# Infini-attention with a token-mixing MLP on one core: block-diagonal memory by wide products, head factors by constant masks, and all engine orders written anew

## The chip, the core and the metric

The kernel runs on one core of a Trainium2 chip. A core has five engines with queues of their own, each strictly in order: TensorE (PE) multiplies matrices into PSUM, VectorE (DVE) and ScalarE (ACT) work on PSUM and SBUF, GpSimd (POOL) on SBUF alone, and SyncE (SP) issues transfers here. Engines wait for each other by semaphores. The metric is the device time of one execution in microseconds (us); a median of several runs is compared.

## The reference

There are S = 2048 tokens of width D = 448. A gate g = sigmoid(x . gate_w) mixes an attention branch a and an MLP branch b for each token. Cut to what matters:

```python
# a: 16 heads of 28, 4 segments of 512 tokens, a running memory M, z for each head
for s in range(4):
    p = softmax(qs @ ks.T * scale + causal_mask)
    a_dot = p @ vs
    a_mem = (phi(qs) @ M) / (phi(qs) @ z + 1e-6)       # phi(t) = t + 1 if t > 0 else exp(t)
    outs.append(gh * a_mem + (1 - gh) * a_dot)         # gh = sigmoid(beta), one factor for a head
    M, z = M + phi(ks).T @ vs, z + sum(phi(ks))
a = concat(outs) @ wo
# b: LayerNorm over D, then an MLP that mixes tokens (S -> 1792 -> S)
u = gelu(h.T @ w1 + b1);  b = (u @ w2 + b2).T
out = g * a + (1 - g) * b
```

## The kernel before

The program records about 1,300 operations with the tiles they read and write, and then puts them on the engines by a table, ORDER, that lists each engine's instructions by name (`word@banks` names the PSUM banks or buffers it takes, `u1-3*2` stands for u1-3 and u1-4, and `#1` is the second operation of that name). Semaphore waits follow from the tiles. So an order that is unlucky costs waits, and never a wrong result.

**Names in the orders.** A number after the name is a tile of 128 tokens, a segment, a head group (4 heads, each in a block of 32 partitions) or an attention unit u = 4 x segment + head group.

- PE: `lo../hi../pr..` are projections of k, q, v (a `lo` and a `hi` use half the rows each; `t` are the v tiles), `sc<p>_<f>` scores of a pair of units in five fills, always in banks 0 to 3; `pv<u>` weights times v; `mst<s>` phi(k).T v of a segment; `mem<u>` phi(q) times the memory; `wo<T>` the output projection; `u<ft>-<st>` and `y<T>-<ft>` the products of the MLP's first and second layer, each of 448 columns, which fill the time between the others.
- ACT: `exp` of four banks at once (L943), `ek/eq` exp of k and q, `cp..` copies out of PSUM (some are on DVE: an operation may have an alternative engine), `gt` the gate's tanh column, `gl` GELU.
- DVE: `pad` copies of weights into padded heads, `bns/bna/vpe/nmr/ln` LayerNorm, `mk/phk` and `mq/phq` the rest of phi, `ta/tm` transposes out of PSUM (L986, L984), `eps/rec/oa/om/ot` the normalised, mixed and transposed attention output, `ev/ag/fin` the exits of the MLP and the output.
- POOL: memsets, `rstd`, `mask` (the causal part of a fill, L946), `o` (the sum of both attention parts, L1001).
- SP: `ld..` loads (ldw1_k_part and ldw2_k_part fill a ring of three weight slots, L554), `dtx` transposing loads of x (L512), `gk/gq` gathers of the heads' last rows through DRAM (24 stores at L731, then `_h` loads at L736, which make up head group 3 of k and q), `tk` the transposes of phi(k) (L757), `out` stores (L1069).

**The memory.** `do_mst` (L808 on) accumulates 128 x 128 sums in one bank; `msta` keeps a running total in float32 (L832, L835), and four `mstc` products (L839) write the four 32 x 32 blocks on the diagonal of each head group's 128 x 128 matrix mst_sb, times a factor maskg, one instruction for each partition block and all four head groups. The rest of mst_sb is zeroed once by `msz0` (L588).

**The head factors.** `do_small` (L843 on) computes gh and 1 - gh from tanh (L860, L862), and for each of the four partition blocks writes a one (`mo`, L866), the gate (`mg`, L867) and the factor for the other part (`oc`, L871): twelve small DVE instructions.

Of the kernel before, what the change touches and what calls it, by code (L numbers as in the profile page):

```python
# [307 lines left out]
y5-13 loq3_2@12 prq3_2 mst2@0 prq3_2h y3-3*3 y6-0@6 y3-6*3 sc6_4@0123 lot12@47 prt12 y6-1 y3-9 prt13 y3-10*2 y6-2
y7-0@4 sc7_0@0123 y7-1 y3-12 y6-3 y3-13 y6-4*2 pv12@7 y6-6 y7-2 sc7_1@0123 y7-3 pv13@5 y7-4 wo8@7 y6-7*2 mem13@5
sc7_2@0123 y6-9*2 y7-5 mem12@7 y6-11 y7-6 wo10@5 y6-12 y7-7 y6-13 sc7_3@0123 y8-0@7*2 wo11@5 y8-2 y10-0@6 y8-3 y7-8  # L310
y8-4 sc7_4@0123 y11-0@5 y7-9 y10-1 y8-5 y7-10*2 y11-1 y10-2 y11-2 y8-6 y10-3 y8-7*2 y9-0@3 y10-4 y7-12*2 wo9@0 y9-1*2
mem15@1 y9-3 y10-5 y9-4*2 y13-0@0 y9-6 y13-1 y11-3 y8-9*2 y10-6*2 y11-4 pv15@4 y9-7*2 pv14@1 y8-11 y10-8 y9-9 y15-0@4
# [8 lines left out]
cpq1_0 cpk1_0 cpq1_1 ek0_0 cpv3 gt3 cpv4 tb cpv5 cpv2 gt5 gt2 cpv1 cpv0 gt4 cpv7 gt6 gt0 gt7 gt1 eq1_0 exp0_0@1 cpk2_2
exp0_1@5 cpk2_1 exp0_2@4 eq1_1 exp0_3@2 exp0_4@6 ek0_2 exp1_0@3 ek0_3 exp1_1@1 eq1_3 exp1_2@5 ek1_0 exp1_3@0 ek1_1
exp1_4@4 gl0 exp2_0@6 exp2_1@1 cpq2_0 exp2_2@5 ek1_3 exp2_3@4 cpq2_2 exp2_4@0 eq2_0 exp3_0@6 ek1_2 exp3_1@2 gl5 gt9
gt8 exp3_2@0 gt11 gt10 exp3_3@3 ek2_0 exp3_4@4 eq2_2 exp4_0@2 exp4_1@5 eq2_1 exp4_2@3 eq2_3 exp4_3@1 exp4_4@6 gl10
exp5_0@0 exp5_1@5 ek2_2 ek2_1 exp5_2@1 eq3_1 exp5_3@2 eq3_0 exp5_4@6 ek2_3 exp6_0@3 exp6_1@4 exp6_2@5 exp6_3@7 cpv15
# [4 lines left out]
cpk0_1#1 gw bna0 maskg0 bna1 bna3 vpe0 cpk0_0#1 cpk0_1 cpq0_1 nmr0 cpq0_3 cpq0_0 bns6 bns4 ln3 bna4 bns7 bns5 bna5  # L330
bns8 bns11 bns10 bna8 bna11 ln1 bna6 bna7 vpe4 bns9 bns14 bna9 bna10 vpe8 ln0 bns15 bns13 nmr8 nmr4 mk0_0 ln4 ln2 cpv6
ln10 ln11 b2c b1c ln8 ln6 ln9 ln5 bns12 mo0 omgh cpk2_3 gh cpq2_3 ln7 mg0 bna13 bna12 bna15 oc0 bna14 oc1 mq1_0 vpe12
phk0_0 mq1_2 nmr12 oc2 ln14 gcol1 ln15 mk0_1 phk0_1 ln12 mo1 ln13 mg1 mo2 cpk2_0 mg2 oc3 ev1 gcol0 phq1_2 ev0 ta0 ev2
omg1 mk0_2 rec0 msz0 ta1 oa0 phk0_2 mq1_1 rec1 phq1_1 phq1_0 mk0_3 mo3 oa1 phk0_3 ev3 ev4 ta2 msta0 mk1_1 ev6 mk1_0
mg3 phk1_1 ot1 omg0 ot0 mq1_3 ta3 ev5 rec2 phk1_0 phq1_3 rec3 mstc0#3 mstc0#2 b2g0 cpq2_1 mstc0#1 mstc0 oa2 oa3 ev8
ev7 ot2 ot3 cpq2_2#1 tm4 mk1_3 eps4 ta4 ag0 rec4 ag2 oa4 ag1 ev9 mq2_0 ag3 mk1_2 cpv8 ta5 cpv9 tm5 phk1_2 eps5 b2g1
phk1_3 cpv11 rec5 om4 cpv10 oa5 tm6 ot4 phq2_0 om5 eps6 gcol2 mk2_0 ta6 rec6 ev10 oa6 phk2_0 tm7 omg2 mq2_2 eps7 om6
ta7 rec7 ev11 ot6 ev13 msta1 ot5 mstc1#3 ev12 om7 oa7 cpk3_1 cpk3_3 cpk3_0 ot7 cpq3_3 cpk3_2 cpq3_1 cpq3_0 mstc1#2 ag5
ag7 ag4 mq2_3 ag6 ta8 mstc1 mstc1#1 phq2_2 mq2_1 tm8 phq2_1 ta9 mk2_1 eps8 phk2_1 b2g2 rec8 oa8 phq2_3 tm9 om8 eps9
mk2_2 fin0 rec9 mq3_0 oa9 fin2 mk2_3 phk2_2 om9 phk2_3 ta10 fin1 tm11 tm10 ot8 eps11 ta11 fin4 ot9 mq3_1 phq3_0 eps10  # L340
cpv14 rec11 om11 oa11 fin5 rec10 msta2 om10 oa10 mstc2#1 cpv12 cpv13 ot10 ot11 mstc2#3 mstc2#2 mstc2 fin3 phq3_1 ta12
ta13 ag8 tm13 tm12 mq3_2 ag10 eps13 fin6 eps12 ag11 rec13 mq3_3 rec12 oa12 om13 oa13 om12 phq3_3 ag9 tm15 fin7 phq3_2
ta15 ot13 eps15 rec15 ta14 tm14 om15 eps14 rec14 oa14 om14 oa15 gcol3 ot15 omg3 b2g3 ot12 fin8 fin9 ot14 fin11 fin10
ag13 fin13 fin12 ag14 fin14 fin15 fin15#1
# [850 lines left out]
```

## Time and profile before

| what | value |
|---|---|
| median of 3 runs | 176.4 us (176.24 to 176.82) |
| the profiled execution | 176.64 us |
| its span, first to last instruction | 174.9 us |
| granted TensorE clock | 1.0 |
| ScalarE's exp of a fill, 40 times | 1.88 us each, 75.0 us |
| DMA moved | 24.66 MB, 141 GB/s on average |

Engine busy times overlap, so they don't add up to the span; what an engine's idle time is worth depends on who waits for it. Lines of the profile read: line of the kernel, engine, operation, output<-input, shape, count, then busy us and mean ns, then idle time before and who ended it.

### The profile page before, as it was taken

Reading aid. Unit: us, or ns where it says so; the run is one execution under the profiler, and the core shown is the slowest. Engines: PE = TensorE matmul, PEld = TensorE weight load, DVE = VectorE, ACT = ScalarE, POOL = GpSimd, SP = SyncE. Lnnn points to the kernel's source line nnn. Section 1 sums busy time; section 2 is a strip of 40 time slices with the busy share of each in tenths; the row PEclk is TensorE's granted clock in tenths of the full one; section 3 lists DMA queues with packets and bytes.
Section 4 is the critical chain, followed back from the end, with each engine's and each line's share of the span. In section 5 each row is a group of like instructions: output and inputs, shape, how many; then the busy total and the mean of one; then the engine's idle time right before and its main releaser. Section 6 shows DMA issues by size and latency. Waiting matters only on the chain.

```text
span 174.9 us, 5948 instructions
## 1 busy us (share of the span) xinstructions
PE 168.6 (96%) x2558; PEld 82.7 (47%) x2558; DVE 144.4 (83%) x336; ACT 118.9 (68%) x122; POOL 64.8 (37%) x93
## 2 busy tenths in 40 slices
PE   8799999999899999999999999999999999999993
PEld 3455444444346444454445344444454445565552
DVE  1788999899814997989897999998899889777963
ACT  2216998984899888999989897997667775000020
POOL 8020120653073005441745370856546242802200
PEclk9999999999999999999999999999999999999999
DMA  5989968948628974401256950047462651246133
GB/s 134 295 155 319 221 155 243 236 125 227 178 37 242 165 174 115 117 14 34 53 155 171 287 42 4 4 70 204 114 190 73 209 179 40 85 141 181 34 110 108
DMA packets 50474, 24.66 MB, mean 141 GB/s; under 512 B 14976, under 2 KB 50208, under 8 KB 50448
## 3 DMA queue, kind: packets, MB, share of 16 engines
q1 hardware_dynamic: 50160, 24.05, 54.5%
q8 instruction: 20, 0.33, 0.8%
q10 hardware_dynamic: 288, 0.23, 0.5%
q14 instruction: 6, 0.05, 0.1%
HBM read 18.76 MB, written 2.36 MB: 121 GB/s over the span
## 4 chain that ended last, share of the span: by engine, by line
PE 82%; DVE 11%; DMA 3%; issue 1%; SPq 1%
PE t L264 71%; PE t L934 6%; PE t L970 4%; DMA t<-in_A_x_dram 3%; DVE t L1007 2%; DVE t L1049 2%; DVE t L709 1%; PE t L819 1%; DVE t L720 1%; DVE t L986 1%; DVE t L839 1%; DVE t L1065 1%; SPq L502 0%; DVE t L614 0%; DVE t L779 0%
## 5 line engine op out<-in xcount | busy, mean ns | idle before, releaser
L264 PE MATMUL t<-t 128*32 128x448 bf16 (+9 forms) x1824 | 144.8, 346 | 0.9 <-DVE t L986 0.3
L264 PEld LDWEIGHTS t<-t 128*32 128x32 bf16 (+2 forms) x1824 | 66.9, 96 | 63.2 <-issue 11.0
L943 ACT ACTIVATE t<-t 128x2048 bf16<-128x2048 f32 x40 | 75.0, 1876 | 15.3 <-PE t L934 14.1
L946 POOL TENSOR_SCALAR_AFFINE_SELECT t<-t 128x512 bf16<-128x512 bf16 x64 | 42.7, 687 | 47.8 <-ACT t L943 46.9
L1001 POOL TENSOR_TENSOR t<-t 128x448 bf16<-128x448 f32 x12 | 14.3, 1197 | 27.2 <-DVE t L999 10.1
L934 PE MATMUL t<-t 28*128 28x512 bf16 (+3 forms) x256 | 15.8, 301 | 0.7 <-issue 0.7
L1027 ACT ACTIVATE t<-t 128x448 bf16<-128x448 f32 x2 | 1.4, 723 | 22.1 <-PE t L264 22.1
L1049 DVE TENSOR_SCALAR t<-t 128x448 bf16<-128x448 f32 x14 | 9.3, 662 | 7.8 <-PE t L264 7.8
L986 DVE STREAM_TRANSPOSE t<-t 128x512 f32<-128x512 f32 x16 | 11.1, 700 | 3.4 <-PE t L970 3.4
L1065 DVE SCALAR_TENSOR_TENSOR t<-t 128x448 bf16<-128x448 f32 (+2 forms) x17 | 10.8, 644 | 3.0 <-PE t L264 2.6
L885 POOL TENSOR_TENSOR t<-t 128x4 f32<-128x4 f32 x4 | 4.5, 1126 | 23.5 <-DVE t L883 23.5
L876 DVE BATCH_NORM_STATS2 t<-t 128x6 f32<-128x448 bf16 x16 | 9.3, 612 | 3.5 <-DMA t<-in_A_x_dram 3.5
L1007 DVE STREAM_TRANSPOSE t<-t 128x512 bf16<-128x512 bf16 x16 | 10.9, 693 | 1.2 <-POOL t L1001 1.2
L934 PEld LDWEIGHTS t<-t 28*128 28x128 bf16 x256 | 4.5, 92 | 15.4 <-ACT t L943 10.9
L1031 DVE TENSOR_SCALAR t<-t 128x448 bf16<-128x448 f32 x14 | 10.1, 736 | 1.9 <-PE t L264 1.9
L970 PE MATMUL t<-t 128*32 128x512 bf16 (+3 forms) x256 | 11.5, 299 | 0.0
L984 DVE STREAM_TRANSPOSE t<-t 128x512 f32<-128x512 f32 x12 | 8.4, 706 | 1.9 <-PE t L264 1.5
L970 PEld LDWEIGHTS t<-t 128*32 128x32 bf16 x256 | 6.8, 96 | 5.1 <-issue 0.4
L779 DVE SCALAR_TENSOR_TENSOR t<-t 128x512 bf16<-128x512 bf16 x12 | 9.0, 755 | 0.0
L997 DVE SCALAR_TENSOR_TENSOR t<-t 128x448 f32<-128x448 f32 x12 | 8.9, 742 | 0.1
L754 DVE SCALAR_TENSOR_TENSOR t<-t 128x512 bf16<-128x512 bf16 x12 | 8.2, 685 | 0.1
L774 ACT ACTIVATE t<-t 128x512 bf16<-128x512 bf16 x12 | 7.5, 626 | 0.7 <-DMA t<-spare_heads 0.7
(65 smaller groups left out, 122.5 us busy)
## 6 DMA issues: line engine op xcount, KB each, us to landing
t<-in_B_w_dram SPq DMA_DIRECT2D x52, 256.0 KB, 3.8
out_dram<-t SPq DMA_DIRECT2D x15, 112.0 KB, 3.0
t<-in_A_x_dram SPq DMA_DIRECT2D x3, 448.0 KB, 5.0
t<-in_B_w_dram SPq DMA_DIRECT2D x8, 128.0 KB, 2.7
t<-in_A_wo_dram SPq DMA_DIRECT2D x4, 98.0 KB
t<-in_A_wq_dram SPq DMA_DIRECT2D x1, 336.0 KB, 5.2
t<-in_A_wv_dram SPq DMA_DIRECT2D x1, 336.0 KB, 5.5
spare_heads<-t SPq DMA_DIRECT2D x8, 32.0 KB
```

Of the source, the lines that this page charges most:

```text
L264: last = e.matmul(out[q], w[:, q], x, skip_group_check=True, **kw)
L876: op("DVE", lambda e: e.bn_stats(st6[:, t, :], xh[:, t, :]), reads=[R_x[t]], writes=[R_st6[t]], name=f"bns{t}", cost=512, prio=P_PROJ - 10 ...
L934: last = e.matmul(bank(fb[hl])[:, c0 : c0 + w], kT[r, hg, s * 512 + j * 128 : s * 512 + j * 128 + 128], qT[r, hg, s * 512 + 128 * j : s * ...
L943: op("ACT", lambda e: e.activation(pslot(g), ps[:, fb[0].bank : fb[0].bank + 4, :], ACT.Exp, scale=SCALE), use=fb, reads=[bres(b) for b in ...
L946: op("POOL", lambda e, c0=c0: e.affine_select(pslot(g)[:, :, c0 : c0 + 128], pslot(g)[:, :, c0 : c0 + 128], pattern=[[0, 4], [1, 128]], co ...
L970: last = e.matmul(bank(cb)[32 * hl : 32 * hl + 32, 128 * j : 512], vaug[:, 4 * s + j, 32 * h : 32 * h + 32], pslot(P_fill[u // 2][f])[:, h ...
L986: dv(lambda e: e.transpose(t2[:, 0, :], bank(cb)[:, 0:512]), [bres(cb)], [R_tt[tb][0]], "ta", 630, use=(cb,))
L1001: op("POOL", lambda e: e.tensor_tensor(o3, n3[0], n3[1], op=ALU.add), reads=R_tt[tb], writes=[R_ob[tb]], name=f"o{u}", cost=1280, port=Tru ...
L1007: dv(lambda e: e.transpose(oT[:, hg, s * 512 : s * 512 + 512], o), [R_ob[tb]], qres(hg, s), "ot", 635)
L1031: alt=("DVE", lambda e: e.tensor_scalar(ag(T), bank(b)[:, 0:D], gcol[:, T : T + 1], b2g[:, T : T + 1], op0=ALU.mult, op1=ALU.add), dve_cos ...
L1049: alt=("DVE", lambda e: e.tensor_scalar_add(uT[:, ft, :], bank(b)[:, 0:D], b1c[:, ft : ft + 1]), dve_cost(448)))
L1065: op("DVE", lambda e: e.scalar_tensor_tensor(outst[:, p, c0:c1], bank(b)[:, 0 : c1 - c0], omg[:, T : T + 1], ag(T)[:, c0:c1], op0=ALU.mult ...
```

## The change

1. **Wide products.** maskg becomes a 128 x 4 x 4 x 32 tile that is zero off the diagonal blocks. Each `mstc` becomes one product of 128 x 512 that writes all of mst_sb for the segment, zeros too: `mstc0` straight from PSUM, `mstc1` and `mstc2` from the float32 total. `msz0` goes. mem waits for one instruction instead of four.
2. **Masks.** POOL builds a constant hmask (three memsets and two selections); `gm` and `osl` multiply the tanh column by it, `oc` becomes one reduction, `mg` one broadcast copy and `mo` one copy.
3. **Alternatives.** `pad`, `ln`, `mg` and `mo` may now run on ACT. In the new table padk1, padq0, padq1, ln1, ln11 and mo do; other copies out of PSUM change sides in both directions.
4. **One more buffer** for exp's results: NP from 5 to 6.
5. **All five orders** are new. The stem of each is as it was; SP's first 19 entries are the same.

The diff, cut to its core (the orders by the parts that are spoken of below):

```diff
     "PE": """
-warm@2 trx0_0@63 warm2 trx0_1@24 lok0_0@71 hik0_0 lok0_2@53 lok0_0h@20 hik0_2 hik0_0h loq0_1@67 gtr@4 lox0_3@03 hiq0_1
+warm@4 trx0_0@13 warm2 trx0_1@52 lok0_0@46 hik0_0 lok0_0h@25 lok0_2@07 hik0_0h loq0_1@13 hik0_2 lox0_3@52 gtr@4 hiq0_1
...
+sc1_0@0123 u3-6 u2-8 u3-7 u2-9 u3-8 u4-0@5 u2-10*2 u3-9 u4-1 u5-2 sc1_1@0123 u2-12 u5-3 u2-13 u4-2*2 u3-10 u2-14 u4-4
...
-u5-13 loq3_2@12 prq3_2 mst2@0 prq3_2h y3-3*3 y6-0@6 y3-6*3 sc6_4@0123 lot12@47 prt12 y6-1 y3-9 prt13 y3-10*2 y6-2
+sc7_0@0123 y7-3*2 y6-5 mst2@5 y6-6 pv12@7 y6-7 sc7_1@0123 y7-5 pv13@5 wo8@7 y6-8*4 y7-6 sc7_2@0123 y7-7 mem12@7 y7-8
...
     "ACT": """
-ldx1 ldwkb xTcp0_01 xTcp0_11 cpk0_2#1 cpk0_2 cpk0_3 cpq0_2 cpq1_2 cpk1_3 cpq1_3 ek0_1 cpk1_2 cpq1_2#1 cpk1_1 eq1_2
+ldx1 ldwkb padk1 xTcp0_01 xTcp0_11 padq1 cpk0_1 padq0 cpk0_1#1 cpk0_0 ek0_0 ek0_1 cpq1_2 ln1 cpq0_1 cpk1_2 cpk1_3
...
+cpk2_2 exp0_0@2 ln11 exp0_1@1 exp0_2@0 ek0_2 eq1_0 exp0_3@5 exp0_4@6 exp1_0@4 ek0_3 exp1_1@2 exp1_2@3 eq1_3 exp1_3@7
...
     "DVE": """
-bns0 padx2 wo0 xTcp0_00 padk0 padk1 padx1 padx0 padk2 bns2 xTcp0_10 bns1 cpk0_0 padq1 padq2 bna2 padq3 padq0 bns3 ob0
+bns0 ob0 padx2 xTcp0_00 maskg0 padx1 padk2 wo0 padx0 padk0 bna0 bns2 xTcp0_10 padq2 padq3 bns1 bna2 cpk0_0#1 bna1
...
+ln15 ln14 ln12 ln13 phk0_1 mq1_2 ev0 ev1 ta0 mk0_2 mq1_0 gcol1 phq1_1 mk0_3 phk0_3 rec0 mg phq1_2 ev2 phk0_2 oc oa0
...
-cpv14 rec11 om11 oa11 fin5 rec10 msta2 om10 oa10 mstc2#1 cpv12 cpv13 ot10 ot11 mstc2#3 mstc2#2 mstc2 fin3 phq3_1 ta12
+oa10 om10 mq3_0 cpq3_2 fin5 cpv14 om11 oa11 b2g2 cpv13 cpv12 fin3 mq3_1 ot11 msta2 ot10 ta12 phq3_0 mstc2 ag8 phq3_1
...
     "SP": """
-gk0_2 ldw1_3_0 gq0_1 ldw1_1_3 tk0_0 ldw1_3_1 gq0_3 tk0_1 gk0_1 ldw1_2_2 gk2_1 ldw1_2_1 ldw1_3_2 gk0_h0 gq0_h2 gk0_h1
-ldw1_2_3 gq0_h1 ldw1_3_3 ldwo3 gk2_0 gq0_h0 tk0_2 ldw1_4_1 tk0_3 ldw1_4_3 ldw1_4_0 ldw1_5_0 ldw1_4_2 ldw1_6_0 dtx3_0
+ldw1_0_0 dtx2_0 dtx2_1 ldw1_1_0 ldw1_0_1 gq0_3 gk0_2 gq0_0 gq0_2 ldwo0 ldw1_0_2 gk0_0 ldw1_0_3 gk0_3 gq0_1 tk0_0
+ldw1_3_0 ldw1_2_0 ldw1_2_1 gk0_1 gq0_h1 ldw1_1_1 gq0_h2 gq0_h0 ldw1_1_2 ldw1_2_2 tk0_1 ldwo2 gk2_0 gk2_2 gk0_h0 gk0_h1
+ldw1_1_3 gk2_3 ldw1_3_3 ldw1_4_1 ldw1_4_0 ldw1_3_1 tk0_3 gk2_1 ldw1_5_0 ldw1_2_3 ldw1_3_2 ldwo3 tk0_2 ldw1_4_2
...
+ldw2_1_3 gq2_h1 ldw2_2_0 ldw2_1_1 ldw2_2_2 gk3_0 ldw2_2_3 tk2_0 ldw2_3_0 ldw2_2_1 out0 ldw2_3_1 gk3_2 gk3_1 tk2_3 out2
...
-    NSL, NP = 3, 5
+    NSL, NP = 3, 6
...
-    maskg = sb([128, NHG, 32], F32)
+    maskg = sb([128, NHG, 4, 32], F32)
...
         if s == 0:
+            op("DVE", lambda e: e.tensor_tensor(diag(), wide(mps()), maskg[:], op=ALU.mult), use=(b,), ...
             op("DVE", lambda e: e.tensor_copy(mst_f32[:], mps()), ...
         else:
             op("DVE", lambda e: e.tensor_tensor(mst_f32[:], mps(), mst_f32[:], op=ALU.add), ...
-        for hl in range(4):
-            q = slice(32 * hl, 32 * hl + 32)
-            op("DVE", lambda e, q=q: e.tensor_tensor(mst_sb[q, s, :, q], mst_f32[q, :, :], maskg[q, :, :], op=ALU.mult), ...
+            op("DVE", lambda e: e.tensor_tensor(diag(), wide(mst_f32), maskg[:], op=ALU.mult), ...
...
+        for w, (v_, n_) in enumerate(((1.0, "hm0"), (0.5, "hm1"), (-0.5, "hm2"))):
+            dv(lambda e, w=w, v_=v_: e.memset(hmask[:, w], v_), [], [R_hmask], n_, "POOL")
...
+        for w, dst, r, n_ in ((1, gsel, R_gsel, "gm"), (2, osel, R_osel, "osl")):
+            dv(lambda e, w=w, dst=dst: e.scalar_tensor_tensor(dst[:], gh[:, :], 1.0 if w == 1 else -1.0, ...
+        dv(lambda e: e.tensor_reduce(omcol[:, :], ...
```

`wide(ap)` repeats the 128 x 4 x 32 input over the four blocks of a row, and `diag()` is mst_sb of the segment seen as 128 x 4 x 4 x 32.

More of the change, by code (lines that the diff above doesn't have):

```diff
@@ L308 @@
[L308 to L312, printed above, removed]
@@ L321 @@
[L321 to L325, printed above, removed]
@@ L330 @@
[L330 to L344, printed above, removed]
+bns0 ob0 padx2 xTcp0_00 maskg0 padx1 padk2 wo0 padx0 padk0 bna0 bns2 xTcp0_10 padq2 padq3 bns1 bna2 cpk0_0#1 bna1
@@ L476, in build_kernel @@
     R_v = R("v", NT)
-    R_mst = [R(f"mst{i}_", 4) for i in range(3)]
-    R_msz = R("msz")
+    R_mst = R("mst", 3)
     R_mstf, R_maskg = R("mstf"), R("maskg")
@@ L585, in build_kernel @@
     op("POOL", lambda e: e.memset(mhalf[:], -0.5), writes=[R_mhalf], name="mhalf", cost=200)
-    for t_, r_, n_, w_ in ((wo_sb, R_wo, "wo0", 896), (mst_sb, [R_msz], "msz0", 768), (maskg, [R_maskg], "maskg0", 128)):
+    for t_, r_, n_, w_ in ((wo_sb, R_wo, "wo0", 896), (maskg, [R_maskg], "maskg0", 512)):
         op("DVE", lambda e, t_=t_: e.memset(t_[:].bitcast(U32), 0), writes=r_, name=n_, cost=w_ / 0.96 + 10, prio=P_PROJ)
@@ L829, in mps, with wide, diag @@
             return bank(b)[:, 0:128].rearrange("p (g c) -> p g c", g=NHG)
+        def wide(ap):
+            return ap[:, :, None, :].to_broadcast([128, NHG, 4, 32])
+        def diag():
+            return mst_sb[:, s].rearrange("p g (l c) -> p g l c", c=32)
         if s == 0:
+            op("DVE", lambda e: e.tensor_tensor(diag(), wide(mps()), maskg[:], op=ALU.mult), use=(b,),
+               reads=[bres(b), R_maskg], writes=[R_mst[0]], name="mstc0", cost=dve_cost(512), prio=P_BASE)
             op("DVE", lambda e: e.tensor_copy(mst_f32[:], mps()), use=(b,), reads=[bres(b)], writes=[R_mstf], name="msta0",
@@ L836, in do_mst @@
                writes=[R_mstf], name=f"msta{s}", cost=dve_cost(128), prio=P_BASE)
-        for hl in range(4):
-            q = slice(32 * hl, 32 * hl + 32)
-            op("DVE", lambda e, q=q: e.tensor_tensor(mst_sb[q, s, :, q], mst_f32[q, :, :], maskg[q, :, :], op=ALU.mult),
-               reads=[R_mstf, R_maskg, R_msz], writes=[R_mst[s][hl]], name=f"mstc{s}", cost=dve_cost(128) + 10, port=True,
-               prio=P_BASE)
+            op("DVE", lambda e: e.tensor_tensor(diag(), wide(mst_f32), maskg[:], op=ALU.mult),
+               reads=[R_mstf, R_maskg], writes=[R_mst[s]], name=f"mstc{s}", cost=dve_cost(512), port=True, prio=P_BASE)
     def do_small():
@@ new lines, in do_small @@
+        for base, step in ((0, -32), (DH - 1, 32)):
+            dv(lambda e, base=base, step=step: e.affine_select(
+                hmask[:], hmask[:], pattern=[[0, 3], [0, NHG], [step, 4]], compare_op=ALU.is_ge, fill=0.0, base=base,
+                channel_multiplier=-1 if base else 1), [R_hmask], [R_hmask], "hs" + str(base), "POOL")
+        for w, dst, r, n_ in ((1, gsel, R_gsel, "gm"), (2, osel, R_osel, "osl")):
+            dv(lambda e, w=w, dst=dst: e.scalar_tensor_tensor(dst[:], gh[:, :], 1.0 if w == 1 else -1.0, hmask[:, w].rearrange("p g l -> p (g l)"),
+                                                              op0=ALU.add, op1=ALU.mult), [R_gh, R_hmask], [r], n_)
@@ new lines, in do_small @@
+        dv(lambda e: e.tensor_reduce(omcol[:, :], osel[:].rearrange("p (g l) -> p g l", l=4), axis=mybir.AxisListType.X,
+                                     op=ALU.add), [R_osel], [R_omcol], "oc")
+        for n_, io, rd in (
+            ("mg", lambda: (maskg[:, :, :, 0:DH], gsel[:].rearrange("p (g l) -> p g l", l=4)[:, :, :, None].to_broadcast([128, NHG, 4, DH])), R_gsel),
+            ("mo", lambda: (maskg[:, :, :, DH], hmask[:, 0]), R_hmask),
+        ):
+            op("DVE", lambda e, io=io: e.tensor_copy(*io()), reads=[rd, R_maskg], writes=[R_maskg], name=n_, cost=550 if n_ == "mg" else 100,
+               prio=pr, alt=("ACT", lambda e, io=io: e.activation(*io(), ACT.Copy), act_cost(448 if n_ == "mg" else 16, True)))
```

130 lines of the change are left out of this document (71 added, 59 removed).

## The prediction

> **What bounds the kernel now.** I read the page first: the span, the busy shares, the chain that ended last, the costliest groups.
>
> ```profile
> span 174.9 us, 5948 instructions
> PE 168.6 (96%) x2558; PEld 82.7 (47%) x2558; DVE 144.4 (83%) x336; ACT 118.9 (68%) x122; POOL 64.8 (37%) x93
> ...
> PE 82%; DVE 11%; DMA 3%; issue 1%; SPq 1%
> ...
> L264 PE MATMUL t<-t 128*32 128x448 bf16 (+9 forms) x1824 | 144.8, 346 | 0.9 <-DVE t L986 0.3
> ```
>
> TensorE is busy for 96% of the span and holds 82% of the chain; the change removes no matrix product (617 entries in PE's order before and after, the same names). So it can win only what TensorE does not fill. The windows of PE alone say where that is (window, length, busy, count, clock, DMA share, GB/s):
>
> ```profile
> 5.00:10.00 5.00, 3.88 (x53) 1.00 1.07 292
> 10.00:15.00 5.00, 4.71 (x55) 1.00 0.87 199
> 45.00:50.00 5.00, 4.34 (x32) 1.00 0.60 119
> 60.00:70.00 10.00, 9.94 (x108) 1.00 0.65 156
> 100.00:110.00 10.00, 9.88 (x189) 1.00 0.33 39
> 130.00:140.00 10.00, 9.68 (x166) 1.00 0.46 134
> 140.00:170.00 30.00, 30.00 (x576) 1.00 0.38 112
> ```
>
> Between 10 and 170 us PE idles 0.29 + 0.66 + 0.06 + 0.12 + 0.32 = 1.45 us, and in the last 30 us not at all. The gap in 5:10 is the wait for x (both orders issue those loads alike). A record hides part of each gap, so I measured the pace of starts. The group by form, then PE's timeline in two windows:
>
> ```profile
> L264 PE MATMUL t<-t 128*128 128x448 bf16 x214 | 46.6, 353 | 0.0
> ```
>
> ```profile
> 155.73 10.53 PE L264 MATMUL t<-t 128*32 128x448 bf16 x224
> ```
>
> ```profile
> 31.98 2.25 PE L264 MATMUL t<-t 128*128 128x448 bf16 x11
> 34.16 0.40 PE L934 MATMUL t<-t 28*128 28x512 bf16 x4
> 34.49 2.31 PE L264 MATMUL t<-t 128*128 128x448 bf16 x11
> ```
>
> 224 quarter products are 56 whole ones: 10.53 / 56 = 0.188 us each, while one record shows 0.353, so a gap of n shown stands for n + 0.165. A score of 512 columns should take 0.188 x 512 / 448 = 0.215; its start-to-start is 34.49 - 34.16 = 0.33. So a change of the array's tile shape costs 0.115 us. Counting shapes in the two order tables gives 97 changes before and 95 after.
>
> **The gaps, and what the change does to each.** (1) At the start, the timeline of 10.6 to 11.6:
>
> ```profile
> 10.68 0.48 DVE L565 MEMSET t<- 128x512 uint32 x1
> ...
> 11.08 0.36 DVE L709 CAST t<-t 128x256 bf16<-128x256 f32 x1
> ...
> 11.50 0.39 PE L264 MATMUL t<-t 64*128 64x512 bf16 x2 [0.29 <-DVE t L709]
> ```
>
> PE waits for a projection's bank, which DVE empties only after the memset ob0. Afterwards ob0 is second on DVE, that copy (the second cpk0_1) runs on ACT, and two products stand between the bank's filling and its reuse. The gap, 0.29 + 0.165 = 0.45, goes. What is late next: the copies of x for the third block (dtx2), wanted earlier, and ACT, which before the first exp gains three pads and one normalisation (ln1) and loses one exp (eq1_0) and some copies. I take 0.3 of 0.45; bounds -0.3 to 0.45.
>
> (2) At 46 us; SP's timeline, then all engines:
>
> ```profile
> 43.67 0.47 SPq L736 DMA_DIRECT2D t<-spare_heads  x1
> ```
>
> ```profile
> 44.25 1.86 ACT L943 ACTIVATE t<-t 128x2048 bf16<-128x2048 f32 x1
> ...
> 46.80 0.63 ACT L774 ACTIVATE t<-t 128x512 bf16<-128x512 bf16 x1 [0.69 <-DMA t<-spare_heads]
> ...
> 46.86 0.40 PE L934 MATMUL t<-t 28*128 28x256 bf16 x8 [0.66 <-issue]
> ```
>
> The exp that held the score banks ended at 46.11, yet both the score of unit 3 and ACT's eq1_3 start at 46.8: both read head group 3 of q, which the transfer gq0_h0 brings from DRAM, issued only at 43.67. It stood right behind gk2_0 in SP's order; now it stands five entries ahead of it, with gk0_h0 and gk0_h1 soon behind. Gain 0.66 + 0.165 - 0.115 (the change that is there anyway) = 0.71. I take 0.7; bounds 0 to 0.71.
>
> (3) At 137 us, DVE's timeline and PE's row:
>
> ```profile
> 135.31 0.88 DVE L839 TENSOR_TENSOR t<-t 32x128 bf16<-32x128 f32 x3
> ...
> 137.46 1.30 DVE L986 STREAM_TRANSPOSE t<-t 128x512 f32<-128x512 f32 x2
> ```
>
> ```profile
> 138.22 0.56 PE L264 MATMUL t<-t 128*32 128x448 bf16 x8 [0.32 <-DVE t L986]
> ```
>
> PE waits for a bank that ta12 empties; before it DVE wrote three of the four diagonal blocks, 0.88 us. Now mstc2 is one instruction and stands behind ta12. The gap, 0.32 + 0.165 = 0.49, goes. What is late next is mem12, which reads mstc2: mst2 is 6.2 us of product time later in PE's order and mem12 only 0.35 later (columns counted in both tables at the pace above). From mst2 to mem12, DVE has msta2 0.25, two transposes 1.4, phq3_0 0.68, mstc2 0.7: 3.0 us, against 3.9 us of products. I take 0.5; bounds 0 and 0.5.
>
> (4) Smaller waits on DVE: 0.06 and 0.12 shown, and others that the records hide. The list of waits:
>
> ```profile
> PEld t L264 <- DVE t L1049: 1.1, 4, 0.4
> ```
>
> Weight loads wait there four times and at a few more lines once or twice; five gaps hidden by 0.165 each and the 0.18 shown make 1.0 us at most. Whether they go hangs on DVE's load, so I price that. The rows by line:
>
> ```profile
> L839 DVE TENSOR_TENSOR t<-t x12: 236/282/289, 62.8 to 135.9; 32x128 bf16<-32x128 f32 x12
> ```
>
> ```profile
> L835 DVE TENSOR_TENSOR t<-t x2: 227/252/278, 96.0 to 130.6; 128x128 f32<-128x128 f32 x2
> ```
>
> ```profile
> L999 DVE TENSOR_TENSOR t<-t x12: 561/616/795, 81.6 to 158.7; 128x448 f32<-128x448 f32 x12
> ```
>
> ```profile
> L867 DVE COPY t<-t x4: 199/213/525, 29.6 to 57.7; 28x112 f32<-28x112 f32 x4
> ```
>
> ```profile
> L871 DVE COPY t<-t x4: 125/160/166, 29.9 to 37.7; 32x4 f32<-32x4 f32 x4
> ```
>
> ```profile
> L588 DVE MEMSET t<- x3: 165/698/805, 4.4 to 41.9; 128x896 uint32 x1, 128x128 uint32 x1, 128x768 uint32 x1
> ```
>
> The wide product is not in the trace. From 128 to 448 elements a product grows by (616 - 252) / 320 = 1.14 ns an element, so 512 take 0.69 us (ends: 0.28 if as a block, 0.795 as the longest of 448). Removed: 12 blocks x 0.28 = 3.4; four mg 1.15, four oc 0.61, msz0 0.70; two gate halves (the price of an oc each) and four tiny memsets 0.6 together: 6.4. Added: three wide 2.1; maskg's memset grows from 128 to 512 elements, 0.84 ns each, 0.3; mg whole, 448 elements (0.25 to 0.74; taken 0.55); gm, osl and the sum oc, 16 elements each, at 0.2: 3.6. DVE loses 2.8 of 144.4 us; the swaps with ACT balance (about 6 us each way). Of the 1.0 us I take 0.3; bounds 0 and 1.0.
>
> (5) Two changes of shape fewer: 0.2. (6) At nothing: POOL's five mask instructions (16 to 48 elements, under 0.3 each) lie in its free time before 12 us; the sixth buffer for exp (NP) lets ACT run ahead, and ACT is not the bound; ACT's 1.2 us more (pads, ln1, ln11, mo) lies in its 32% of idle time, except that ln11 waits for nmr8 with exp0_1 and so the third score behind it.
>
> Gains: 0.3 + 0.7 + 0.5 + 0.3 + 0.2 = 2.0 us.
>
> **What the new order adds.** Every queue is reshuffled, so new gaps come. Before, an order of this kind had some ten gaps, 2.6 us. I see tight places: sc0_0 (ACT's last gate column about 0.1 late by my estimate), ln11, mem12 (0.9 to spare), and SP's queue:
>
> ```profile
> SPq L757 <- DVE t L754: 10.0, 2, 8.7
> ```
>
> ```profile
> L757 SPq DMA_TRANSPOSE t<-t x12: 1190/1228/3255, 31.4 to 122.5; - x12
> ```
>
> ```profile
> DMA to landing us min/median/max: 2.2/3.6/6.8
> ```
>
> (the last for L554, the weights). SP's transposes of phi(k) wait for DVE, longest 8.7 us, and what stands behind waits too. tk0_1 used to stand after ldw1_1_3; now ldw1_1_3 stands six entries behind tk0_1 (ldwo2, gk2_0, gk2_2, gk0_h0 and gk0_h1 between): 1.23 + 2.5 us of issues, then 3.6 to land. I put all new gaps together at 1.0 us; ends 0 and 3.1 (the slower rival below).
>
> **Sum.** The profiled execution took 176.64 us: span 174.9 and 1.7 around it, which the change leaves. 176.64 - 2.0 + 1.0 = 175.6. That execution is 0.24 above the median of the runs, 176.4; on the median the forecast is **175.4**.
>
> **Rivals.** *Nearly all is won*: new gaps of 0.2 or less: 176.4 - 1.8 = 174.6. For it: DVE lighter by 2.8. Against: the margins above are under 1 us.
>
> *Taken back elsewhere*: the gaps move, 2.0 new for 2.0 gone: 176.4. The likeliest place is the meeting of DVE and POOL:
>
> ```profile
> L995 DVE TENSOR_SCALAR t<-t x12: 142/172/615, 70.7 to 157.5; 128x16 f32<-128x16 f32 x12
> ```
>
> An instruction of 172 ns took 615: 0.44 lost, four or five such meetings in places that matter make 2.0. The Trainium skill, "SBUF — State Buffer", Who interferes with whom, says that a DVE instruction with two SBUF inputs contends with a GpSimd instruction that reads SBUF, and that whichever comes first keeps the pair for its whole length. By that rule mstc1 and mstc2, wide and with two such inputs, could each wait out a mask; the row of L839, the same kind in small, has 289 as its longest and bears no sign of it, while that of L995 agrees.
>
> *Slower: a weight behind a transpose.* ldw1_1_3 feeds u2-12, right behind the second score of pair 1. In the chain of waits that score is
>
> ```profile
> 43.50 0.33 PE t L934 x8
> ```
>
> and 1.1 us fewer products stand ahead of it now; with 0.3 won at the start it comes near 42. phk0_1, which releases tk0_1, and its neighbour on DVE:
>
> ```profile
> 34.04 0.69 DVE L754 SCALAR_TENSOR_TENSOR t<-t 128x512 bf16<-128x512 bf16 x1
> ...
> 34.65 0.71 DVE L892 TENSOR_SCALAR t<-t 128x448 bf16<-128x448 bf16 x1
> ```
>
> It ended at 34.73; afterwards 5.7 us of rows that stood ahead of it stand behind or elsewhere and 2.2 come ahead (two normalisations, copies), but DVE waits for PE in between, so I estimate 33.75. Then the weight lands at 33.8 + 3.7 + 3.6 = 41.1, 0.9 before its use: from 34.7 on, or with a landing above 4.5 of the 2.2 to 6.8, every 0.1 us late is 0.1 of PE. Two meetings with POOL (0.71 for a normalisation of 0.39 is one: 0.3) and a landing 1.0 longer make 0.6 + 1.0 - 0.9 = 0.7 of gap; the same pattern at two more transposes (tk0_3 before ldw1_2_3, tk2_0 before ldw2_2_1) makes 2.1 in all: 176.4 - 1.0 + 2.1 = 177.5.
>
> *The change doesn't do what it says*: if the wide products cost 0.795 and mg 0.74, DVE still loses 2.3; the case lies inside the forecast.
>
> **Chances.** Forecast (174.9 to 175.9) 0.40; nearly all won 0.20; taken back 0.22; slower 0.18. About 0.3% (0.53 us) is what a measurement of this kernel can tell from no change. Forecast and full gain lie beyond it: 0.60 faster; of "taken back", centred on no change, nearly all is within: 0.21; slower 0.19. The range from 174.0 to 177.2 cuts the lower edge of the full gain and the upper half of the slower case.
>
> **What would show it.** Right: no PE gap at 11 us, none with a release by the gather near 46, none before wo8; L839's successors three at about 0.69; DVE's busy time near 141.6; PE idle in 10 to 170 near 0.7 us. Wrong: a PE gap released by a DMA of L554 near 42 us, SP waiting longest on L754's successor; exp0_1 late behind ln11; mem12 late behind mstc2; POOL or DVE instructions at twice their usual length just before a PE gap.

## The result and the profile after

The changed kernel takes **175.17 us** in the median of 20 runs (174.49 to 176.5), the kernel before 176.51 us beside it (20 runs). The ratio is 0.9936 (95% interval 0.9911 to 0.996): 0.4 to 0.9% faster. The forecast was 175.4. The profiled execution took 175.05 us, against 176.64 before.

The page of the changed kernel: span, busy times, chain, and the largest group on TensorE.

```profile
span 173.3 us, 5628 instructions
PE 166.6 (96%) x2401; PEld 83.3 (48%) x2408; DVE 143.0 (83%) x314; ACT 120.2 (69%) x125; POOL 64.6 (37%) x98
...
PE 79%; ACT 5%; DMA 5%; DVE 4%; SPq 3%; issue 1%
...
L264 PE MATMUL t<-t 128*32 128x448 bf16 (+11 forms) x1667 | 143.0, 345 | 1.8 <-issue 0.9
```

TensorE is as full as before, and its shown idle time between 10 and 169 us is not less in this execution: 1.70 us, where it was 1.45 (0.7 had been named as the sign). The chain passes through DVE with 4% in place of 11, and through ACT, DMA and SP with 13%. DVE fell from 144.4 to 143.0 us, half of the 2.8 expected; ACT gained 1.3. The windows of TensorE (window, length, busy, count, clock, DMA share, GB/s):

```profile
5.00:10.00 5.00, 3.97 (x53) 1.00 1.11 311
10.00:15.00 5.00, 4.24 (x49) 1.00 0.87 242
...
40.00:50.00 10.00, 9.63 (x105) 1.00 0.83 220
60.00:70.00 10.00, 9.95 (x106) 1.00 0.38 95
100.00:110.00 10.00, 9.95 (x162) 1.00 0.11 26
130.00:140.00 10.00, 9.95 (x197) 1.00 0.37 107
```

130 to 140 holds 0.05 of idle time where it held 0.32. But 10 to 15 holds 0.76, where it held 0.29, and 40 to 50 holds 0.37. The timeline says why, first at 13.67, then at 42.90 (start, duration, engine, line, operation; in brackets the idle time before it and what ended it):

```profile
9.16 1.15 SPq L513 DMA_TRANSPOSE t<-in_A_x_dram  x1
...
13.67 0.59 PE L264 MATMUL t<-t 64*128 64x256 bf16 x7 [0.76 <-issue]
...
34.29 1.21 SPq L762 DMA_TRANSPOSE t<-t  x1
...
38.85 0.40 SPq L555 DMA_DIRECT2D t<-in_B_w_dram  x1
...
42.90 0.55 PE L264 MATMUL t<-t 128*128 128x448 bf16 x2 [0.36 <-DMA t<-in_B_w_dram]
```

The first is loq1_2, which reads the transposed x that dtx1_1 (issued at 9.16, landed at 13.58) brings. The second is u2-12, which reads the weight ldw1_1_3 (38.85), behind the transpose tk0_1 (34.29): the slower rival's mechanism. The same two rows by their landings (the views of each line, in the window of its issue): dtx1_1 took 4.4 us from issue to landing, where it took 2.8 before, and ldw1_1_3 took 4.0.

```profile
L513 SPq DMA_TRANSPOSE t<-in_A_x_dram x1: 1153/1153/1153, 9.2 to 9.2; - x1
...
DMA to landing us min/median/max: 4.4/4.4/4.4
...
L555 SPq DMA_DIRECT2D t<-in_B_w_dram x1: 403/403/403, 38.9 to 38.9; - x1
...
DMA to landing us min/median/max: 4.0/4.0/4.0
```

**Start to start.** Records overlap, so I compare starts of products, product by product along PE's order. Three numbers are used below. *x* is the start of PE's second transposition of x (line 640 before, 645 after), which waits for the second load of x. *W* is from there to the start of the last product. A *gap* is what one start-to-start exceeds the product's own pace, with 0.115 us for a change of tile shape taken off. For the profiled execution before, x = 7.08, last product 171.74, W = 164.7; after, 6.61, 169.89 and 163.3. So of the 1.85 us between the two last products, 0.48 is x alone, which no part of the change touches, and 1.37 lies in W. These are two single executions:

| gap | before | after |
|---|---|---|
| lox0_3, at 11 us | 0.45 | 0 |
| loq1_2, at 13.7 us (dtx1_1) | 0 | 0.95 |
| u2-12, at 42.9 us (ldw1_1_3) | 0 | 0.43 |
| sc1_2, at 46 us (gq0_h0) | 0.71 | 0 |
| wo8, at 137 us | 0.49 | 0 |
| smaller ones of 0.08 to 0.27: eight before, four others after | 1.19 | 0.50 |

All excesses together are 5.57 us before and 4.42 after; what the table leaves out (2.73 and 2.54) is about 0.3 behind each of the three `mst` and otherwise hundredths. Two changes of shape fewer give 0.23: 5.57 - 4.42 + 0.23 = 1.38, which is the fall of W.

### The profile page after: what moved, and what is told of

It is laid out like the page before. It is cut to its first block, busy times and chain, and to the rows that moved or that the text cites. A ratio compares the mean times of both kernels' runs of the same rounds, so it can differ in the third digit from the quotient of the medians.

```text
span 173.3 us, 5628 instructions
## 1 busy us (share of the span) xinstructions
PE 166.6 (96%) x2401; PEld 83.3 (48%) x2408; DVE 143.0 (83%) x314; ACT 120.2 (69%) x125; POOL 64.6 (37%) x98
## 4 chain that ended last, share of the span: by engine, by line
PE 79%; ACT 5%; DMA 5%; DVE 4%; SPq 3%; issue 1%
PE t L264 67%; PE t L949 6%; PE t L985 4%; DMA t<-in_A_x_dram 3%; DMA t<-in_B_w_dram 2%; ACT t L794 1%; ACT t L772 1%; ACT t L712 1%; DVE t L905 1%; SPq L736 1%; ACT t L723 1%; PE t L824 1%; DVE t L1022 1%; ACT t L779 1%; SPq L762 1%
## 5 line engine op out<-in xcount | busy, mean ns | idle before, releaser
L264 PE MATMUL t<-t 128*32 128x448 bf16 (+11 forms) x1667 | 143.0, 345 | 1.8 <-issue 0.9
L264 PEld LDWEIGHTS t<-t 128*32 128x32 bf16 (+2 forms) x1674 | 67.8, 96 | 62.9 <-issue 11.3
L961 POOL TENSOR_SCALAR_AFFINE_SELECT t<-t 128x512 bf16<-128x512 bf16 x64 | 41.7, 670 | 53.6 <-ACT t L958 52.8
L1012 DVE SCALAR_TENSOR_TENSOR t<-t 128x448 f32<-128x448 f32 x12 | 8.2, 681 | 0.0
L1014 DVE TENSOR_TENSOR t<-t 128x448 f32<-128x448 f32 x12 | 8.1, 680 | 0.0
```

Of the source, the lines that this page charges most:

```text
L264: last = e.matmul(out[q], w[:, q], x, skip_group_check=True, **kw)
L961: op("POOL", lambda e, c0=c0: e.affine_select(pslot(g)[:, :, c0 : c0 + 128], pslot(g)[:, :, c0 : c0 + 128], pattern=[[0, 4], [1, 128]], co ...
```

## The experiments

The ratios are to the kernel before on the same chip, with 95% intervals. Each order of a mixed kernel is that of the kernel named, with the small instructions of the other form put where those that they replace stood.

**The same two kernels again.** Were the gaps at 13.7 and 42.9 the price of the new orders, or of one execution? No edit.

> The changed kernel as it is, beside the others on one chip. Ratio to before 0.991 to 0.996. Its second profile tells whether the gap of 0.95 us ahead of loq1_2 (waiting for the transposed x of block 1, dtx1_1, landed 13.58) belongs to the order or to that one execution: if to the order, dtx1_1 lands after 13.3 again and the gap is over 0.5 us; if to the execution, it lands near 12 and the gap is under 0.3. The gap of 0.43 us ahead of u2-12 (weights ldw1_1_3) should return within 0.3 us either way.

> The changed kernel once more. Ratio 0.989 to 0.994; from the second transpose of x to the last product 162.1 to 162.6 when dtx1_1 and ldw1_1_3 land in time, up to 163.3 when they don't; no gap above 0.1 ahead of loq2_0, which is the product's share: a_order2b minus this is 0.6 to 1.0 us.

> The kernel before, against itself: what this comparison takes for a difference where there is none. Ratio 0.997 to 1.003. Its profile is the second of before: if the time from the second transpose of x to the last product is a property of the order, it is 164.4 to 165.1 us again (first profile 164.65); if the gap of 0.54 ahead of u1-12 that the other old-order runs show is a race between DVE and POOL, it may appear here too, without any change of the kernel.

The changed kernel: 0.9892 (0.9857 to 0.9926) and 0.99 (0.9864 to 0.9935), on two other chips, 1.9 us between the medians in both; the kernel before against itself 1.0008 (0.9985 to 1.003). All waits of PE in the first repeat of the changed kernel, in its list of waits (engine, line <- what it waited for: us, times, longest):

```profile
PE t L645 <- DMA t<-in_A_x_dram: 1.9, 1, 1.9
PE t L604 <- PEq L1195: 0.8, 1, 0.8
```

No wait is listed after the start; the gap at 42.9, which I expected again, did not return. dtx1_1 was issued at 10.00 and took 2.9 us, ldw1_1_3 was issued at 38.44 and landed 2.9 later, at 41.4, 1.1 ahead of the 42.47 at which u2-12 could have started in the execution shown above:

```profile
10.00 1.16 SPq L513 DMA_TRANSPOSE t<-in_A_x_dram  x1
...
12.34 2.13 PE L264 MATMUL t<-t 64*128 64x512 bf16 x22
...
38.44 0.41 SPq L555 DMA_DIRECT2D t<-in_B_w_dram  x1
...
42.27 0.40 PE L949 MATMUL t<-t 28*128 28x384 bf16 x8
42.60 0.74 PE L264 MATMUL t<-t 128*128 128x448 bf16 x3
```

W is 162.2 in both repeats, against 163.3 in the first execution, and 164.5 in the repeat of the kernel before. So the two gaps are not in the order as such: they are margins of under 1.2 us which a late transfer uses up in one execution of three. Neither gap stands in the three executions of the old code in the same order of SP (further on); dtx1_1 took 2.8 to 2.9 us there. That the repeats are hardly faster in total (175.35 and 174.83, against 175.05) comes from outside W: x was 0.9 later in both, and from the last product's start to the end of the execution they took 5.7 and 5.1 us, against 5.2.

**Each half alone.** The new code in the old orders, with NP = 5, on two chips. (The sixth buffer and the work moved to ACT count with the new orders here.) Here mstc0 is taken from the copied total, since the old order has msta0 first. DVE's order:

```diff
-... phk0_1 ln12 mo1 ln13 mg1 mo2 cpk2_0 mg2 oc3 ev1 gcol0 phq1_2 ev0 ta0 ev2 omg1 mk0_2 rec0 msz0 ta1 ...
+... phk0_1 ln12 ln13 cpk2_0 ev1 gcol0 phq1_2 ev0 ta0 ev2 omg1 mk0_2 rec0 ta1 ...
-... msta2 om10 oa10 mstc2#1 cpv12 cpv13 ot10 ot11 mstc2#3 mstc2#2 mstc2 fin3 phq3_1 ta12 ...
+... msta2 om10 oa10 mstc2 cpv12 cpv13 ot10 ot11 fin3 phq3_1 ta12 ...
```

> The wide products and the constant masks in the old orders (mstc0 from the total instead of PSUM). Theory: DVE's load is what TensorE waited for between 95 and 138 us, so the lighter DVE shortens those gaps without any new order: DVE busy 2.5 to 3 us less, the gap ahead of wo8 (0.49) gone, ratio 0.996 to 0.998. Rival: the orders alone made the gain; ratio 0.9985 to 1.0015 and the gaps move.

> The kernel of b_code once more (new code, old orders), beside the other three corners on one chip. Theory (the new orders hold the larger part, since DVE's time is worth little where the order does not use it): ratio 0.996 to 0.999, from the second transpose of x to the last product 164.4 to 164.9. Rival (code alone makes the gain, as the 0.9933 of b_code says): ratio 0.992 to 0.995.

And the old code, with its four block products and its twelve small factor instructions, in the new orders; DVE's again:

```diff
-... phk0_3 rec0 mg phq1_2 ev2 phk0_2 oc oa0 ta1 ...
+... phk0_3 rec0 mo0 mg0 mo1 mg1 mo2 mg2 mo3 mg3 msz0 phq1_2 ev2 phk0_2 oc0 oc1 oc2 oc3 oa0 ta1 ...
-... ta12 phq3_0 mstc2 ag8 ...
+... ta12 phq3_0 mstc2 mstc2#1 mstc2#2 mstc2#3 ag8 ...
```

> The new orders with the old four block products and the old twelve small factor instructions (each put where its successor stands). Theory: DVE is 2.5 to 3 us heavier, gaps of 0.4 to 1.0 us in all return between 95 and 140 us, ratio 0.996 to 0.999. Rival (orders alone): ratio 0.992 to 0.995, as the changed kernel on the same chip.

The new code in the old orders: 0.9933 (0.991 to 0.9955), and 0.9954 (0.9928 to 0.9979) on another chip. The old code in the new orders was slower, 1.0042 (1.0016 to 1.0068). Its list of waits, then its DVE and PE around 46:

```profile
PE t L264 <- DVE t L992: 1.3, 2, 0.7
PE t L976 <- DVE t L1055: 0.9, 1, 0.9
```

```profile
43.92 0.21 DVE L871 COPY t<-t 28x112 f32<-28x112 f32 x1
44.20 0.06 DVE L870 MEMSET t<- 28x4 f32 x1
44.29 0.42 DVE L871 COPY t<-t 28x112 f32<-28x112 f32 x1
44.91 0.70 DVE L588 MEMSET t<- 128x768 uint32 x1 [0.20 <-issue]
...
46.24 0.68 DVE L1055 TENSOR_SCALAR t<-t 128x448 bf16<-128x448 f32 x1
...
47.06 0.73 PE L976 MATMUL t<-t 128*32 128x512 bf16 x16 [0.91 <-DVE t L1055]
```

pv1 needs a bank that ev2 (46.24) empties, and ev2 stands behind the small copies and msz0. But I had put them there: eight small instructions and a memset, where the new order has one (mg). So the same old code once more, with msz0, mo0 and mg0 ahead of ev0, the other mo and mg and oc0 ahead of ev1, and oc1 to oc3 ahead of ta0, where DVE has some slack; run twice:

```diff
-... phk0_1 mq1_2 ev0 ev1 ta0 mk0_2 ... rec0 mo0 mg0 mo1 mg1 mo2 mg2 mo3 mg3 msz0 phq1_2 ev2 phk0_2 oc0 oc1 oc2 oc3 oa0
+... phk0_1 mq1_2 msz0 mo0 mg0 ev0 mo1 mg1 mo2 mg2 mo3 mg3 oc0 ev1 oc1 oc2 oc3 ta0 mk0_2 ... rec0 phq1_2 ev2 phk0_2 oa0
```

> As a_order (new orders, old products and factors), but msz0 and the twelve factor instructions stand in idle time of DVE, ahead of ev0, ev1 and ta0 (34 to 40 us). Theory: it is the place that costs, where DVE has no slack; the gaps of 1.1 ahead of pv1 and 0.85 ahead of u6-0 go and those ahead of loq2_0 and after y6-8 (four block products) stay: ratio 0.992 to 0.998. Rival: any added DVE time costs its own length: ratio 1.001 to 1.006, as a_order.

> The kernel of a_order2 once more (old code, new orders, the removed small work placed in DVE's idle time). Theory: ratio 0.993 to 0.997, from the second transpose of x to the last product 163.0 to 163.6, with the gap of 0.67 ahead of loq2_0, behind four block products, again. Rival (orders alone gain nothing): 0.999 to 1.003.

0.9969 (0.9944 to 0.9993) and 0.9937 (0.9914 to 0.996), with the waits at 47 gone. On one chip stand the four together:

| | old orders | new orders |
|---|---|---|
| old code | 1.0008 (0.9985 to 1.003) | 0.9937 (0.9914 to 0.996) |
| new code | 0.9954 (0.9928 to 0.9979) | 0.99 (0.9864 to 0.9935) |

The code alone gives 0.5%, the orders alone 0.6%, both 1.0%: within the intervals they add. On the other chips the halves gave 0.7 and 0.3%. W of the profiled executions splits otherwise: before 164.7 and 164.5, code alone 163.9 and 164.6, orders alone 163.2 and 163.3, both 163.3, 162.2 and 162.2. By W the orders bring 1.3 us and the code 0 to 0.8 in the old orders, but 1.0 in the new ones where no transfer is late. So each half gains, and how the gain divides is known to some tenths of a microsecond only.

Where the code's gain sits can be read. In the new orders, the old code has a gap of 0.6 us ahead of loq2_0, at 59 to 61 us, in each of its three executions: PE waits for the transpose ta2, which stands behind mstc0's four block products. The list of waits of the second placing shows it, and that of the changed kernel has no such row:

```profile
PE t L264 <- DVE t L992: 0.6, 1, 0.6
```

In the old orders the gap before wo8 is gone as soon as mstc2 is one instruction. ta12, which began at 137.46 behind three block products among others, starts at 136.56, and PE runs through (DVE, then PE, of the new code in the old orders):

```profile
136.56 0.71 DVE L998 STREAM_TRANSPOSE t<-t 128x512 f32<-128x512 f32 x1
...
137.06 0.72 PE L982 MATMUL t<-t 128*32 128x512 bf16 x16
137.61 1.71 PE L264 MATMUL t<-t 128*32 128x448 bf16 x32
```

**The gather at 46 us.** One entry of SP moved (six places forward), in the kernel before and in the new code with old orders:

```diff
-... gk0_h0 gq0_h2 gk0_h1 ldw1_2_3 gq0_h1 ldw1_3_3 ldwo3 gk2_0 gq0_h0 tk0_2 ...
+... gk0_h0 gq0_h2 gq0_h0 gk0_h1 ldw1_2_3 gq0_h1 ldw1_3_3 ldwo3 gk2_0 tk0_2 ...
```

> The kernel before with one entry of SP's order moved: the gather gq0_h0 right behind gq0_h2, nine entries earlier. Theory: the gap at 46 us (0.71 us) goes and nothing else moves: no PE gap above 0.2 there, ratio 0.995 to 0.998. Rival: SP waits at gq0_h0 for its stores and the weights behind it come late, so a gap of like size opens between 40 and 46 us; ratio 0.999 to 1.001.

> Wide products and masks in the old orders, with gq0_h0 moved as in b_gq. Theory: the two gains add (DVE's 1.1 us and the gap at 46, 0.7), so this comes to the changed kernel without any of its new orders: ratio 0.987 to 0.991. Rival: the new orders hold a gain of their own beyond that gap; ratio 0.992 to 0.994.

0.9982 (0.9956 to 1.0007), not told from no change, and 0.9975 (0.9951 to 0.9999), no better than the code without it. In the kernel before, the gap at 46 is 0.14 with the move, where the profile of the prediction had 0.71. But that is not shown to be the move's doing, for in the repeat of the kernel before, with gq0_h0 in its old place, the gap is 0.18. PE, then ACT, of that repeat:

```profile
44.71 2.44 PE L264 MATMUL t<-t 128*128 128x448 bf16 x12
47.29 0.40 PE L934 MATMUL t<-t 28*128 28x256 bf16 x8
...
47.22 0.63 ACT L774 ACTIVATE t<-t 128x512 bf16<-128x512 bf16 x1 [0.22 <-DMA t<-spare_heads]
```

By the single records gq0_h0 took 2.5 us there (issued at 44.74, landed at 47.20), and 3.1 in the profile read (43.67 to 46.77). So the size of this gap hangs on how long the transfer takes in an execution. With the new code and the move the gap is 0.89, though gq0_h0 landed 2.7 us ahead of the score. ACT and PE of that kernel:

```profile
41.60 1.88 ACT L955 ACTIVATE t<-t 128x2048 bf16<-128x2048 f32 x1 [1.68 <-PE t L946]
...
44.81 0.63 ACT L754 ACTIVATE t<-t 128x512 bf16<-128x512 bf16 x1 [1.33 <-DMA t<-spare_heads]
...
45.35 1.86 ACT L955 ACTIVATE t<-t 128x2048 bf16<-128x2048 f32 x1
...
47.27 0.40 PE L946 MATMUL t<-t 28*128 28x256 bf16 x8 [0.84 <-ACT t L955]
```

ACT's ek0_3 waits 1.33 us for the other gather, gk0_h1 (issued 40.44, landed 44.74 by the single records), the next exp stands behind ek0_3, and the score needs the bank that this exp empties. In the moved kernel before, whose x came 0.7 later, the same exp starts at 45.43: both kernels run into the same transfer, and what was won ahead of it is waited out there. The interval of the moved kernel before holds both the gain of 0.2 to 0.5% that I expected and none; my theory that the gains add here falls. The new SP order has gk0_h1 at 38.4.

**The wide product alone.** The kernel before with one 128 x 512 product, its mask filled block by block by the old mo and mg, and without msz0:

```diff
-    maskg = sb([128, NHG, 32], F32)
+    maskg = sb([128, NHG, 4, 32], F32)
...
-        for hl in range(4):
...
+        op("DVE", lambda e: e.tensor_tensor(
+            mst_sb[:, s].rearrange("p g (l c) -> p g l c", c=32), mst_f32[:, :, None, :].to_broadcast([128, NHG, 4, 32]),
+            maskg[:], op=ALU.mult), ...
...
-                maskg[q, :, 0:DH],
+                maskg[q, :, hl, 0:DH],
```

> The kernel before with the wide products alone (msz0 gone with them), old factor instructions, old orders. Theory: the gaps between 95 and 138 us hang on the products, so this has most of b_code's gain: the gap ahead of wo8 gone, ratio 0.993 to 0.996. Rival: the factor instructions between 28 and 57 us carry it; ratio 0.998 to 1.001.

0.9988 (0.9964 to 1.0012): its gap before wo8 is gone in the trace too, but the time can't tell it from none. Its interval overlaps that of the whole code on one chip (0.9928 to 0.9979) and not on the other (0.991 to 0.9955), and neither is the chip of this run. The masks alone were not run, so how the code's gain divides between products and masks stays open.

**The two late transfers moved forward.** In the changed kernel, dtx1_1 ahead of ldwo1 and ldw1_1_3 ahead of tk0_1:

```diff
-... dtx1_0 ldwo1 dtx1_1 ldx4 ...
+... dtx1_0 dtx1_1 ldwo1 ldx4 ...
-... ldw1_2_2 tk0_1 ldwo2 gk2_0 gk2_2 gk0_h0 gk0_h1 ldw1_1_3 gk2_3 ...
+... ldw1_2_2 ldw1_1_3 tk0_1 ldwo2 gk2_0 gk2_2 gk0_h0 gk0_h1 gk2_3 ...
```

> The changed kernel with two entries of SP's order moved: dtx1_1 right behind dtx1_0 (ahead of ldwo1, which waits for the load of wv), and ldw1_1_3 ahead of tk0_1. Theory: the two gaps of the changed kernel's first profile (0.95 and 0.43 us) are landings without margin that are late in some executions only; with more margin (dtx1_1 issued near 8.2, ldw1_1_3 near 33) neither shows, and the slower executions become fewer: median 0.1 to 0.5 us under the changed kernel's, ratio 0.986 to 0.991. Rival: those gaps only stand in for an x that came early, and the end doesn't move: ratio 0.989 to 0.993.

0.9931 (0.9903 to 0.9958), not told from the changed kernel (0.9892 to 0.9936 in its own runs), where I had expected 0.986 to 0.991. Neither gap is in its trace (dtx1_1 landed at 12.42, ldw1_1_3 at 38.39), and W is 162.4, as in the repeats where no transfer was late. So the transfers have more margin, but neither time nor W shows that it is worth anything. Its one larger gap, 0.42 us, stands between two products, and nothing that the trace records ended it:

```profile
136.35 1.12 PE L264 MATMUL t<-t 128*32 128x448 bf16 x19
137.71 1.12 PE L264 MATMUL t<-t 128*32 128x448 bf16 x17 [0.25 <-issue]
```

The two moves didn't make it: at the same place, behind y6-8, all seven executions with the new order of TensorE lose time, 0.1 to 0.2 us in the three of the changed kernel and 0.5 in the three with the old code. What it is stays open.

## Why the prediction was right

The time was right, and two terms were too small and nearly cancelled. How close the forecast came, 175.17 to 175.4, is in part luck. The 20 runs of the result lie in two groups, 11 from 174.49 to 175.2 and 9 from 175.78 to 176.5, and the median falls at the edge between them. On the two later chips the medians are 1.9 us apart, which is what "nearly all is won" gave (1.8), where the forecast had 1.0. The steps:

1. *The start, 0.3 of 0.45.* The gap went in full. The late transfer behind it was another than the ones named (dtx2's copies): dtx1_1, and only in one execution of three.
2. *The gather, 0.7.* Right for the changed kernel, which has no gap at 46, but in part by luck. The 0.71 belongs to the one execution that was read: the repeat has 0.18 there and loses 0.54 behind phk0_1 instead (see the last section), a loss that the prediction doesn't count. The new orders lose neither, and that both executions lose about 0.7 in all is chance. The reason given was also half of it: the move of gq0_h0 alone leaves the score behind gk0_h1 through ACT. The new order moves both.
3. *wo8, 0.5.* Right, and in the traces shown without the orders: one instruction in place of four is enough. mem12, named as next late, shows no gap.
4. *Smaller waits, 0.3 of 1.0.* Mis-sized. The eight gaps add to 1.19, and went; the 0.5 of smaller ones that came in their place belongs to the term of new gaps. DVE's lighter load, by which I had measured this term, is 1.4 us in place of 2.8, so it doesn't account for the gaps that went; which of the moves do isn't separated. The price of the code was not the error: in the old orders it takes DVE from 144.4 and 145.1 us (the repeat) to 142.0 and 142.2, in the new ones from 146.4 and 146.3 to between 143.0 and 143.8. Wrong was that the copies changing sides with ACT balance: the new orders put 1.2 to 2.0 us on DVE. The pages of the new code in the old orders and of the old code in the new ones:

```profile
PE 168.4 (96%) x2558; PEld 82.6 (47%) x2558; DVE 142.0 (81%) x317; ACT 119.0 (68%) x122; POOL 66.3 (38%) x98
```

```profile
PE 166.6 (96%) x2401; PEld 82.8 (47%) x2408; DVE 146.3 (84%) x334; ACT 120.1 (69%) x124; POOL 63.8 (37%) x93
```

5. *Two changes of shape, 0.2.* The traces have 97 and 95 changes, so 0.23 at the price of 0.115, which no run measured by itself.

The wide product was priced at 0.69 us by extrapolation. The view of the line of mstc1 and mstc2: 0.68, both times.

```profile
L850 DVE TENSOR_TENSOR t<-t x2: 681/682/682, 97.3 to 136.6; 128x512 bf16<-128x512 f32 x2
```

*What the new order adds, 1.0.* Mis-sized both ways, by the profile that the prediction read. Steps 1 to 4 take 0.45 + 0.71 + 0.49 + 1.19 = 2.84 us off the gaps, and shape 0.23 more, 3.07 against the 2.0 written. W fell by 1.37 in the first profiled execution and by 2.5 and 2.5 in the repeats, so new gaps cost 1.7 in the one and 0.6 in the others. The forecast's net of 1.0 stands against 1.3 of the medians of the result, and 1.9 of the two later ones.

*The rivals.* "Nearly all is won" is what the repeats' W shows, and the medians of 175.2 lie between it and the forecast. The slower rival's place was right: ldw1_1_3 landed at 42.85 in one execution, 1.75 later than the 41.1 estimated: its issue came 1.35 later (0.5 of that is tk0_1's), and it took 4.0 in place of 3.6. In both repeats it landed at 41.4. The two further transposes of that rival showed nothing.

"Taken back where DVE meets POOL" didn't decide the result, but such meetings cost time in the old orders; see below. The row that was said to agree with the rule on two SBUF inputs does not belong under it: L995 adds a constant to one input. Its 615 ns stand beside one of POOL's masks in the trace (they start at 143.48 and 143.43), so it is a meeting all the same.

## What to carry to other kernels

When every queue is reordered, price each half by itself: the same code in the old orders and the old code in the new ones, with the small work put where the engine has slack; here each half was worth 0.3 to 0.7% and neither was the whole. Before pricing a gap, look for it in a second execution of the same kernel: the gap of 0.71 was 0.18 there, and 0.54 stood at another place. After a wait on one transfer is removed, look at every other transfer that the same stage reads before counting the gain, for the stage runs on into the next one. A margin on a transfer has to be judged over several executions: 1.1 us was enough in two of three.

## What the hardware showed that was not expected

**The second load of x.** Its issue is the same in all the programs (2.17 to 2.21 us after the span's start), and yet in the 14 profiled executions it landed between 6.56 and 7.64 us: seven times up to 7.04, seven times from 7.45 on. PE's row that waits for it, in the changed kernel and in its repeat:

```profile
6.61 0.62 PE L645 MATMUL t<-t 128*128 128x128 bf16 x8 [0.96 <-DMA t<-in_A_x_dram]
```

```profile
7.51 0.62 PE L645 MATMUL t<-t 128*128 128x128 bf16 x8 [1.89 <-DMA t<-in_A_x_dram]
```

That is about 1 us in a single execution, near the 1.3 to 1.9 that the change brings, so two profiles alone could not have settled it. Whether this load makes the two groups in the 20 times of the result is not shown, since unprofiled runs have no trace; in the repeats single times lie between the groups (175.35, 175.63).

**A collision decided by a few nanoseconds.** In the kernel before, DVE's phk0_1 and POOL's first causal mask both start at 34.04. DVE takes its usual 0.69, and the mask 1.19, where an undisturbed one takes 0.64. In the repeat of the same kernel both start at 34.50, and it is DVE that loses:

```profile
34.50 1.17 DVE L754 SCALAR_TENSOR_TENSOR t<-t 128x512 bf16<-128x512 bf16 x1
...
34.50 0.64 POOL L946 TENSOR_SCALAR_AFFINE_SELECT t<-t 128x512 bf16<-128x512 bf16 x1 [1.24 <-ACT t L943]
```

With the new code in the old orders and gq0_h0 moved, POOL is first, by 0.07:

```profile
33.91 2.91 POOL L958 TENSOR_SCALAR_AFFINE_SELECT t<-t 128x512 bf16<-128x512 bf16 x4 [0.98 <-ACT t L955]
33.98 1.10 DVE L758 SCALAR_TENSOR_TENSOR t<-t 128x512 bf16<-128x512 bf16 x1
...
35.85 0.92 PE L264 MATMUL t<-t 128*128 128x448 bf16 x4 [0.38 <-DVE t L902]
```

phk0_1 takes 1.10 us, the normalisation ln12 behind it ends late, and PE waits 0.54 us start to start, where the first profile of the kernel before had 0.06. The same 0.54 stands in all six other executions with the old orders, the repeat of the kernel before among them, so the profile that the prediction read is the exception. The Trainium skill, "SBUF — State Buffer", Who interferes with whom, says that such an instruction with two SBUF inputs contends with a GpSimd instruction that reads SBUF, and that the order of issue decides which one waits. The traces agree where the starts are apart: with POOL ahead by 7 ns (the repeat, in the unrounded records) to 78 ns DVE loses 0.41 to 0.48 us. Where POOL is ahead by 1 ns, in the first profile, POOL lost. In all seven executions with the new orders phk0_1 starts about 0.53 ahead of the first mask (33.58 and 34.11 in the changed kernel), takes 0.68, and no gap follows.
